# Retention followed by a squared-ReLU FFN: pacing FFN steps by thirds of a chunk in block 0 and by a line of tokens afterwards

## Chip, cores and metric

One Trainium2 chip, one core of it. The metric is the device time of the whole program in microseconds (us). A *ratio* is the mean time of one kernel's fast runs over the mean of the other's fast runs of the same rounds; it is therefore not quite the ratio of the medians that are quoted beside it. Engine names: PE is TensorE (PEld its weight loads), DVE is VectorE, ACT is ScalarE, POOL is GpSimd, SP issues the transfers. The *granted clock* is the share of PE's full clock that the profile records as granted; *half clock* is 0.50. A *bank* is a buffer of the kernel that PE writes, and that another engine has to read before PE may write it again.

## The reference

```python
# attention: batch 8, heads 8, sequence 576, head dim 64
scores = (q @ k.transpose(0, 1, 3, 2)) / sqrt(64)
ret    = scores * where(rel >= 0, gamma ** rel, 0)      # decay per head
x      = (ret @ v).transpose(0, 2, 1, 3).reshape(4608, 512)
# FFN: w_in 512 x 2048, w_out 2048 x 512
h      = maximum(x @ w_in, 0)
out    = (h * h) @ w_out
```

## The kernel before

Three stages overlap in one instruction stream. *Attention* goes in 40 chunks of up to 128 tokens (per batch four of 128 and one of 64). *The first FFN product* goes in 9 blocks of 512 tokens (`TOK`). Block 0 has 16 plain steps (`first_in`), each four products of 128x512; blocks 1 to 8 have 28 steps each (`ffn_in`) of a seven-product scheme that needs sums of x and of the weights. *The second product* (the output product) comes last, alone. The weights arrive as 64-bit floats and are converted on DVE and ACT, six parts per piece, while block 0 runs.

In these traces PE takes its matmuls in the program's order (it idled 5.36 us before T6 below, with an FFN step behind it whose weights were ready), so the program decides where FFN steps stand between the parts of attention. That is what `ffn`, called three times per chunk (once per *third*), does.

```python
def turn(i):        # transposes k and q of chunk i on PE into the t bank, then copies
    p = ps_t.tile([128, 2, 512], F32, tag="t")          # one buffer
    ...                                                 # 16 transposes
    nc.scalar.copy(to, p[...])                          # kT, ACT
    nc.vector.tensor_tensor(to, p[...], dq[...])        # qT, DVE

def scores(i):      # scores into the same t bank, masked by DVE ("ret")
    ...
    nc.vector.tensor_tensor(r[:cs], both[:cs], msk[...], op=ALU.mult)

def retain_c(i):    # last part of attention of a chunk
    ...
    if more:
        grown(i, 1)                                     # state to SBUF, ACT
    ...
    while at < tok + cs:
        n = at // TOK
        while steps and steps[0][0] <= (n - 2 if n > 4 else n - 3):
            step()                                      # forced: x[n] takes this block's room
            owed[0] -= 1
        ...
        nc.scalar.copy(xT[n][...], p[...])              # x to SBUF, ACT: frees x's bank
        ...                                             # a whole block of x queues its steps

def ffn_in(n, mp, j):                                   # step of blocks 1..8
    if j == 0 and mp == 0:
        for f in sums_x[n]:
            f()                                         # x sums that are still due
    ...                                                 # 4 products of 128x256, then DVE, ACT, POOL
    if mp == N_MP - 1 and j in (3, 4, 5) and n_next[0] > n + 1:
        sums_x[n + 1].pop(0)()                          # one x sum of the next block

def ffn(i):                                             # called per third of a chunk
    if tok < TOK + R_0:                                 # R_0 = 640 tokens
        rate = (N_W1 - 2) / R_0 if tok >= TOK else 0
    elif tok < 5 * TOK:
        rate = (3 * N_MP * NP - LAG) / (4 * TOK - TOK - R_0 + TOK)
    else:
        rate = N_MP * NP / TOK
    owed[0] += cs / 3 * rate
    while steps and owed[0] >= 1:
        owed[0] -= 1
        step()

for i in range(N_CH + 1):                               # the part after the first chunks
    retain_a(i - 1); ffn(i - 1); convert(6)
    retain_b(i - 1)
    scores(i);       ffn(i - 1); convert(6)
    turn(i + 1)
    retain_c(i - 1); ffn(i - 1); convert(6)
```

Of the kernel before, what the change touches and what calls it, by code (L numbers as in the profile page):

```python
# [15 lines left out]
C = 128  # L16
CH = C // 2
TOK = 512
# [22 lines left out]
def kernel(  # L41
# [36 lines left out]
    B, H, S, D = q.shape  # L78
# [7 lines left out]
    N_MP = N_M // 2  # L86
    N_MQ = N_M // 2
    N_BLK = n_tok // TOK
    NP = len(PRODUCTS)
    NCH = -(-S // C)  # L90
    chunks = [(b, ci, ci * C, min(C, S - ci * C)) for b in range(B) for ci in range(NCH)]
    N_CH = len(chunks)
# [62 lines left out]
    N_W1 = N_DF  # L155
# [89 lines left out]
    def w_out_parts():  # L245

        for j in range(N_W1, N_W1 + 3):
            yield lambda j=j: fetch_w(j)
        for j in range(N_W1, len(pieces)):
            one, two, beside, three, four, five = round_parts(j)  # L250
            yield one
            yield lambda two=two, beside=beside: (two(), beside())
            yield three
            yield four

            def last(j=j, five=five):
                five()
                fetch_w(j + 3)

            yield last  # L260
            wi, m, e = pieces[j]
            mh, mq = divmod(m, N_MQ)
            if e == 1:

                at = slice(2 * mh, 2 * mh + 2)
                b = [stage[0][:, o, at, :] for o in range(4)] + [stage[1][:, o, at, :] for o in range(3)]
                r1, r2, r3, r4 = right_sums(*b)
                yield lambda r1=r1, r2=r2: (r1(), r2())
                yield lambda r3=r3, r4=r4: (r3(), r4())
            if e == 1 and mh == 1:  # L270

                for st_, at in ((stage[0], slice(0, 4)), (stage[1], slice(4, 7))):
                    yield from right_sums(*(st_[:, :, o, :] for o in range(NP)))
                    yield lambda st_=st_, at=at, mq=mq: nc.sync.dma_start(
                        w2_dram[at, :, mq, :].rearrange("o p f -> p o f"), st_.rearrange("p o s f -> p o (s f)"))
# [4 lines left out]
    def fetch_raw(count):  # L280

        for _ in range(count):
            if n_raw[0] < min(N_W1, n_made[0] + N_RAW):
                fetch_w(n_raw[0])
                n_raw[0] += 1
# [23 lines left out]
    def convert(count):  # L309
        for _ in range(count):  # L310
            f = next(w_in_steps, None)
            f and f()
# [14 lines left out]
    for half in range(2):  # L327
        at = slice(CH * half, CH * half + CH)
# [8 lines left out]
    N_EARLY = TOK // C  # L337
# [76 lines left out]
    def within(i, h):  # L414

        s = st[i]
        b_, ci, c0, cs = chunks[i]
        own, grow = [], []
        for hp, e, b in HEADS:
            own.append(lambda hp=hp, e=e, b=b: nc.tensor.matmul(  # L420
                x_at(hp, b, h), lhsT=s["vs"][rows(h), 2 * hp + b, :], rhs=s["ret"][rows(h), e, hp, :],
                start=clears(b, hp // 2), stop=False, skip_group_check=True))
            grow.append(lambda hp=hp, e=e, b=b: nc.tensor.matmul(  # L423
                u_ps[0][rows(e), hp, :], lhsT=loaded[i][1][rows(1 - h), 2 * hp + e, :], rhs=s["vs"][rows(1 - h), 2 * hp + b, :],
                start=(ci == 0 and h == 1 and hp == 0), stop=(hp == HP - 1), skip_group_check=True))
        return own, grow

    def grown(i, h):
        nc.scalar.copy(u_sb[(2 * chunks[i][1] + h + 1) % 3], u_ps[0])

    def retain_a(i):

        b_, ci, c0, cs = chunks[i]
        xp[0] = ps_x.tile([128, 2, 256], F32, tag="x", name="x_ps", padded_shape=[128, 2, 512])
        clean.clear()
        if ci == 0:
            u_ps[0] = ps_u.tile([128, HP, D], F32, tag="u", name="u_ps")
        if cs < C:
            return
        own, grow = within(i, 1)  # L440
        for j in range(0, len(own), 2):
            for f in own[j:j + 2] + grow[j:j + 2]:
                f()
        grown(i, 0)

    def retain_b(i):

        s = st[i]
        b_, ci, c0, cs = chunks[i]
        for h in reversed(range(cs // CH)):  # L450
            if 2 * ci + h == 0:
                continue
            u = u_sb[(2 * ci + h) % 3]
            for hp, e, b in HEADS[0:2] + HEADS[4:6] + HEADS[2:4] + HEADS[6:8]:
                nc.tensor.matmul(x_at(hp, b, h), lhsT=u[rows(e), hp, :], rhs=s["qT"][rows(e), hp, CH * h:CH * h + CH],  # L455
                                 start=clears(b, hp // 2), stop=False, skip_group_check=True)

    def retain_c(i):

        b_, ci, c0, cs = chunks[i]  # L460
        own, grow = within(i, 0)
        more = ci + 1 < NCH
        if i < N_EARLY or i >= N_CH - 2:

            nc.scalar.copy(u_sb[(2 * ci + (cs // CH)) % 3][:, 0:2, 0:1], xp[0][:, :, cs - CH:cs - CH + 1])
        for j in range(0, len(own), 2):
            for f in own[j:j + 2] + (grow[j:j + 2] if more else []):
                f()
        if more:
            grown(i, 1)  # L470
        tok = b_ * S + c0
        at = tok
        p = xp[0][:, :, 0:256].rearrange("p a (g t) -> p a g t", g=2)
        while at < tok + cs:
            n = at // TOK

            while steps and steps[0][0] <= (n - 2 if n > 4 else n - 3):
                step()
                owed[0] -= 1
            end = min(tok + cs, (n + 1) * TOK)  # L480
            nc.scalar.copy(xT[n][:, :, at - n * TOK:end - n * TOK].rearrange("p (a g) t -> p a g t", a=2),  # L481
                           p[:, :, :, at - tok:end - tok])
            at = end
            if n_next[0] < N_BLK and (n_next[0] + 1) * TOK <= at:
                steps.extend(block_steps(n_next[0]))
                n_next[0] += 1
        st[i] = loaded[i] = None
# [137 lines left out]


    steps = []
    owed = [0.0]
    w_out_steps = w_out_parts()
    n_w2 = [0]  # L630

    def block_steps(n):
        if n == 0:
            return [(0, first_in, j) for j in range(N_W1)]
        return [(n, ffn_in, n, mp, j) for mp in range(N_MP) for j in range(NP)]

    def step():
        n, f, *args = steps.pop(0)
        f(*args)

    n_next = [0]



    R_0 = TOK * 5 // 4
    LAG = 7

    def ffn(i):

        b, ci, c0, cs = chunks[max(0, min(i, N_CH - 1))]  # L650
        tok = b * S + c0
        if tok < TOK + R_0:
            rate = (N_W1 - 2) / R_0 if tok >= TOK else 0
        elif tok < 5 * TOK:
            rate = (3 * N_MP * NP - LAG) / (4 * TOK - TOK - R_0 + TOK)
        else:
            rate = N_MP * NP / TOK
        owed[0] += cs / 3 * rate
        while steps and owed[0] >= 1:
            owed[0] -= 1  # L660
            step()

    turn(0)
    for i in range(N_CH + 1):
        if i <= N_EARLY:

            convert((0, 0, 2, 5, 5)[i])
            if i >= 1:
                retain_a(i - 1)
                retain_b(i - 1)  # L670
                retain_c(i - 1)
            convert((0, 0, 1, 1, 1)[i])
            if i == N_EARLY:
                step()
            scores(i)
            if i == N_EARLY:
                convert(6)
                step()
            turn(i + 1)
            if i == N_EARLY:  # L680
                convert(5)
        else:
            retain_a(i - 1)
            ffn(i - 1)
            convert(6)
            retain_b(i - 1)
            if i < N_CH:
                scores(i)
            ffn(i - 1)
            convert(6)  # L690
            if i + 1 < N_CH:
                turn(i + 1)
            retain_c(i - 1)
            ffn(i - 1)
            convert(6)
        if i + 3 < N_CH:
            load(i + 3)
        if i < N_EARLY:
            fetch_raw(1)
# [210 lines left out]
```

## Time and profile before

| what | before |
|---|---|
| timed median (1019.52 to 1026.13) | 1025.22 us |
| span of the profiled execution | 1019.0 us |
| PE busy / DVE busy | 983.6 / 751.6 us |
| output product starts, lasts | 616.4, 402.6 us |

PE is busy 97% of the span. The prediction below shows the lines that tell where the rest is. One view is added here: DVE in order of time in the worst place, between two attention transposes without an FFN step (start, length in us, work).

```profile
48.07 0.69 DVE L381 TENSOR_TENSOR qT<-t_ps,dq 128x512 f32<-128x512 f32 x1
48.68 0.42 DVE L205 TENSOR_SCALAR w<-w 128x512 uint32<-128x512 uint32 x1
...
50.79 0.69 DVE L223 SCALAR_TENSOR_TENSOR w<-w,w 128x512 uint32<-128x512 uint32 x1
51.40 0.42 DVE L205 TENSOR_SCALAR w<-w 128x512 uint32<-128x512 uint32 x1
...
53.52 0.69 DVE L223 SCALAR_TENSOR_TENSOR w<-w,w 128x512 uint32<-128x512 uint32 x1
54.13 0.68 DVE L406 TENSOR_TENSOR ret<-sc_ps,msk 128x512 f32<-128x512 f32 x1
```

PE had finished the scores at 49.5. The mask that reads them (L406, "ret") starts only at 54.13, behind two weight conversions (each from L205 to L223); and the next transposes need the bank that the mask frees.

### The profile page before, as it was taken

The page shows a single profiled execution, that of the slowest core. Times are in us where ns is not written, and L with a number is a line of the kernel's source. Part 1 is how long each engine was busy: PE and PEld are TensorE (multiplying, and loading weights), DVE is VectorE, ACT ScalarE, POOL GpSimd, SP SyncE. Part 2 cuts the span into 40 slices and gives each one's busy share as a digit, 9 for nine tenths or more (in the row PEclk, how much of TensorE's full clock was granted, in tenths as well). Part 3 has the DMA queues.
Part 4 walks back from the last instruction along what each step waited for, and adds up shares of the span by engine and source line. Part 5 has one row for each costly group of instructions (what it writes and reads, how often), then busy time and mean ns, then how long its engine had stood idle before and what let it go on. Part 6 is the DMA issues. An engine that isn't in the chain of part 4 may idle for free.

```text
span 1019.0 us, 24086 instructions
## 1 busy us (share of the span) xinstructions
PE 983.6 (97%) x10376; PEld 862.1 (85%) x10376; DVE 751.6 (74%) x1418; ACT 184.9 (18%) x425; POOL 80.3 (8%) x82
## 2 busy tenths in 40 slices
PE   6789999999999999999999998999999999999998
PEld 4444488888888788888788888999999999999997
DVE  2679577666888887888886776877777677777765
ACT  2435221111312213212221000000000000000000
POOL 1100001101111011110101000000000000000000
PEclk9789999999999999999999999999999999999999
DMA  8965547737578669669537898784855747565351
GB/s 201 236 191 162 131 154 204 195 122 208 159 241 270 188 227 268 219 211 288 178 146 271 337 420 307 279 288 157 290 201 200 271 167 258 193 232 207 124 207 42
DMA packets 187658, 220.34 MB, mean 216 GB/s; under 512 B 119200, under 2 KB 137632, under 8 KB 178592
## 3 DMA queue, kind: packets, MB, share of 16 engines
q1 hardware_dynamic: 187552, 218.81, 65.8%
q8 instruction: 81, 1.33, 0.5%
q14 instruction: 25, 0.20, 0.1%
HBM read 129.39 MB, written 89.39 MB: 215 GB/s over the span
## 4 chain that ended last, share of the span: by engine, by line
PE 90%; DVE 4%; DMA 2%; SPq 2%; issue 1%; ACT 1%; DVEq 0%; ACTq 0%
PE h_b L578 17%; PE o_b L790 16%; PE h_c L578 11%; PE h_a L578 11%; PE o_c L790 11%; PE o_a L790 11%; PE h_ps L543 5%; PE x_ps L420 3%; PE t_ps L373 2%; PE x_ps L455 2%; PE sc_ps L399 1%; DMA a<-g_dram 1%; DMA k_ld<-in_k_dram 1%; PE u_ps L423 1%; SPq L142 1%
## 5 line engine op out<-in xcount | busy, mean ns | idle before, releaser
L578 PE MATMUL h_b<-room,w 128*128 128x256 f32 x736 | 178.0, 385 | 0.0
L578 PEld LDWEIGHTS h_b<-room,w 128*128 128x128 f32 x736 | 136.5, 190 | 19.9 <-DVE room L597 0.3
L790 PE MATMUL o_b<-w,room 128*128 128x128 f32 x1168 | 144.5, 275 | 0.2 <-DVE room L741 0.2
L790 PEld LDWEIGHTS o_b<-w,room 128*128 128x128 f32 x1168 | 137.2, 192 | 0.5 <-DVE room L741 0.4
L790 PE MATMUL o_c<-w,room 128*128 128x128 f32 x1008 | 123.0, 275 | 0.0
L790 PEld LDWEIGHTS o_c<-w,room 128*128 128x128 f32 x1008 | 117.7, 192 | 0.0
L578 PE MATMUL h_c<-room,w 128*128 128x256 f32 x480 | 115.9, 384 | 0.0
L578 PE MATMUL h_a<-room,w 128*128 128x256 f32 x448 | 106.9, 381 | 0.0
L578 PEld LDWEIGHTS h_c<-room,w 128*128 128x128 f32 x480 | 89.2, 190 | 12.8
L578 PEld LDWEIGHTS h_a<-room,w 128*128 128x128 f32 x448 | 84.3, 190 | 12.2 <-issue 0.5
L790 PE MATMUL o_a<-w,a 128*128 128x128 f32 x688 | 85.9, 275 | 2.6 <-DMA a<-g_dram 2.6
L790 PEld LDWEIGHTS o_a<-w,a 128*128 128x128 f32 x688 | 81.3, 192 | 2.9 <-issue 2.8
L585 DVE SCALAR_TENSOR_TENSOR room<-room 128x512 f32<-128x512 f32 x96 | 69.7, 726 | 3.3
L595 POOL TENSOR_TENSOR room<-room 128x512 f32<-128x512 f32 x32 | 35.9, 1121 | 441.8 <-ACT room L594 358.7
L801 ACT COPY r<-o_a 128x128 f32<-128x128 f32 x54 | 14.4, 266 | 276.9 <-PE o_a L790 246.3
L543 PE MATMUL h_ps<-room,w 128*128 128x512 f32 x128 | 62.7, 636 | 1.0 <-ACT room L481 1.0
L420 PEld LDWEIGHTS x_ps<-ret,v_ld 64*64 64x64 f32 x1152 | 42.4, 143 | 20.1 <-issue 13.6
L597 DVE TENSOR_TENSOR room<-h_b,room 128x512 f32<-128x512 f32 x32 | 22.1, 691 | 50.1 <-PE h_b L578 47.7
L420 PE MATMUL x_ps<-ret,v_ld 64*64 64x64 f32 x1152 | 52.6, 234 | 5.7 <-ACT room L481 1.9
L408 POOL TENSOR_TENSOR v_ld<-v_ld,dv 128x512 f32<-128x512 f32 (+1 forms) x40 | 44.2, 1108 | 90.3 <-DMA v_ld<-in_v_dram 69.7
L543 PEld LDWEIGHTS h_ps<-room,w 128*128 128x128 f32 x128 | 24.5, 201 | 28.0 <-issue 25.7
L588 ACT COPY room<-h_a 128x512 f32<-128x512 f32 x32 | 18.8, 587 | 157.4 <-PE h_a L578 157.4
(94 smaller groups left out, 1361.1 us busy)
## 6 DMA issues: line engine op xcount, KB each, us to landing
g_dram<-room SPq DMA_DIRECT2D x32, 1792.0 KB, 7.3
a<-g_dram SPq DMA_DIRECT2D x43, 1024.0 KB, 6.8
room<-g_dram SPq DMA_DIRECT2D x20, 1024.0 KB, 6.0
w<-w_dram SPq DMA_DIRECT2D x7, 1792.0 KB, 12.2
out_dram<-room SPq DMA_DIRECT2D x18, 512.0 KB, 3.3
v_ld<-in_v_dram SPq DMA_DIRECT2D x32, 256.0 KB, 3.8
w<-in_moe_w_in_dram SPq DMA_DIRECT2D x16, 512.0 KB, 5.0
w<-in_moe_w_out_dram SPq DMA_DIRECT2D x16, 512.0 KB, 3.8
```

Source lines behind the costliest of these rows:

```text
L373: nc.tensor.transpose(p[:, h, j, hp, :], loaded[i][j][rows(h), 2 * hp:2 * hp + 2, :], ident[rows(h), rows(h)])
L408: nc.gpsimd.tensor_tensor(vs[:cs], vs[:cs], dv[:cs, :, ci:ci + 1].to_broadcast([cs, H, D]), op=ALU.mult)
L420: own.append(lambda hp=hp, e=e, b=b: nc.tensor.matmul(x_at(hp, b, h), lhsT=s["vs"][rows(h), 2 * hp + b, :], rhs=s["ret"][rows(h), e, hp, : ...
L455: nc.tensor.matmul(x_at(hp, b, h), lhsT=u[rows(e), hp, :], rhs=s["qT"][rows(e), hp, CH * h:CH * h + CH], start=clears(b, hp // 2), stop=Fa ...
L543: nc.tensor.matmul(p.rearrange("p h t -> p (h t)"), lhsT=w[:, c, :], rhs=xT[0][:, c, :], start=(c == 0), stop=(c == N_DM - 1))
L578: nc.tensor.matmul(p[:, mm, :], lhsT=w[:, c, :], rhs=xs[n][right][:, c, :], start=(j in OPENS and mm == 0 and c == 0), stop=(j in CLOSES a ...
L585: nc.vector.scalar_tensor_tensor(t, t, 0.0, t, op0=ALU.max, op1=ALU.mult)
L588: nc.scalar.copy(p1, p)
L595: nc.gpsimd.tensor_tensor(g["A11"], g["A11"], g["A11"], op=ALU.mult)
L597: nc.vector.tensor_tensor(g["A22"], p, p15, op=ALU.add)
L790: nc.tensor.matmul(p, lhsT=s["lefts"][left][:, m, :], rhs=w_out[j][:, m, WO_SLOT[right], :], start=(i in OPENS and m == 0), stop=(i in CLO ...
L801: nc.scalar.copy(r[:, 0, 0:128], p)
```

## The change

The intent: in block 0 exactly one FFN step and one conversion per third, so that no third is without a step; after that a line of (tokens, steps) points that finishes each block about when its x room is wanted, again with at least one step in each third. The copy of x also goes ahead of the copy of the state on ACT, to free x's bank sooner.

```diff
-        if more:
-            grown(i, 1)
         tok = b_ * S + c0
...
             nc.scalar.copy(xT[n][:, :, at - n * TOK:end - n * TOK]...)
+            if more and at == tok:
+                grown(i, 1)
...
+    THIRD = C // 3
+    PACE = ((4 * TOK + THIRD // 2, N_W1 + 2 * N_MP * NP - 2), (5 * TOK - THIRD, N_W1 + 3 * N_MP * NP - 2),
+            (6 * TOK + THIRD // 2, N_W1 + 4 * N_MP * NP - 2), (8 * TOK + THIRD // 2, N_W1 + 6 * N_MP * NP - 2),
+            (9 * TOK, N_W1 + 7 * N_MP * NP - 2))
...
     def ffn(i):
...                                              (the three rates and `owed` are gone)
+        gone[0] += chunks[max(0, min(i, N_CH - 1))][3] / 3
+        if steps and steps[0][0] == 0:
+            step()
+            return
...                                              (want: the line's value at gone[0])
+        if steps:
+            step()
+        while steps and done[0] < int(want):
             step()
```

More of the change, by code (lines that the diff above doesn't have):

```diff
@@ L478, in retain_c @@
                 step()
-                owed[0] -= 1
             end = min(tok + cs, (n + 1) * TOK)
@@ L627 @@
     steps = []
-    owed = [0.0]
     w_out_steps = w_out_parts()
@@ L638, in step @@
         n, f, *args = steps.pop(0)
+        done[0] += 1
         f(*args)
     n_next = [0]
-    R_0 = TOK * 5 // 4
-    LAG = 7
-    def ffn(i):
-        b, ci, c0, cs = chunks[max(0, min(i, N_CH - 1))]
-        tok = b * S + c0
-        if tok < TOK + R_0:
-            rate = (N_W1 - 2) / R_0 if tok >= TOK else 0
-        elif tok < 5 * TOK:
-            rate = (3 * N_MP * NP - LAG) / (4 * TOK - TOK - R_0 + TOK)
-        else:
-            rate = N_MP * NP / TOK
-        owed[0] += cs / 3 * rate
-        while steps and owed[0] >= 1:
-            owed[0] -= 1
+    THIRD = C // 3
+    PACE = ((4 * TOK + THIRD // 2, N_W1 + 2 * N_MP * NP - 2), (5 * TOK - THIRD, N_W1 + 3 * N_MP * NP - 2),
+            (6 * TOK + THIRD // 2, N_W1 + 4 * N_MP * NP - 2), (8 * TOK + THIRD // 2, N_W1 + 6 * N_MP * NP - 2),
+            (9 * TOK, N_W1 + 7 * N_MP * NP - 2))
+    done = [0]
+    gone = [0]
+    behind = []
+    def ffn(i):
+        gone[0] += chunks[max(0, min(i, N_CH - 1))][3] / 3
+        if steps and steps[0][0] == 0:
+            step()
+            return
+        if not behind:
+            behind.append((gone[0] - THIRD, done[0]))
+        points = behind + [p for p in PACE if p[0] > behind[0][0]]
+        want = points[-1][1]
+        for (x0, y0), (x1, y1) in zip(points, points[1:]):
+            if gone[0] < x1:
+                want = y0 + (y1 - y0) * (gone[0] - x0) / (x1 - x0)
+                break
+        if steps:
+            step()
+        while steps and done[0] < int(want):
             step()
@@ L682 @@
         else:
+            if i == N_EARLY + 1:
+                gone[0] = TOK
             retain_a(i - 1)
```

## The prediction

> **What bounds the kernel now.** I read the page's busy line first, then the table by stage, the waits of the matmul engine (PE), and last its order of time where the waits fall. All times are us from the start of the profiled span of 1019.0 (that execution took 1020.7; the timed median is 1025.22). The page:
>
> ```profile
> PE 983.6 (97%) x10376; PEld 862.1 (85%) x10376; DVE 751.6 (74%) x1418; ACT 184.9 (18%) x425; POOL 80.3 (8%) x82
> PE   6789999999999999999999998999999999999998
> DVE  2679577666888887888886776877777677777765
> PEclk9789999999999999999999999999999999999999
> ```
>
> PE is the bound, and the change gives it not one matmul more or less. So only three things can be won: PE's idle time, PE's time at a lower clock, and small gaps that the busy figure hides. Slices 2 and 3 (25 to 76 us) show a granted clock of 0.7 and 0.8. The table by stage (stretch, its length, busy us of each engine with instruction counts, granted clock, DMA share, GB/s):
>
> ```profile
> 47.40:61.20 13.80, 7.43 (x87) 4.53 (x86) 11.80 (x23) 4.11 (x8) 1.07 (x1) 0.63 0.79 220
> 61.20:111.90 50.70, 48.34 (x572) 24.27 (x570) 39.44 (x64) 22.21 (x43) 4.94 (x4) 1.00 0.55 155
> 111.90:136.20 24.30, 22.91 (x267) 14.90 (x268) 12.43 (x20) 5.80 (x12) 0.00 (x0) 1.00 0.61 161
> 136.20:550.00 413.80, 409.34 (x4993) 341.87 (x4993) 330.35 (x546) 97.03 (x193) 58.67 (x54) 1.00 0.67 205
> 550.00:616.40 66.40, 66.40 (x320) 58.22 (x321) 48.47 (x72) 6.60 (x13) 6.24 (x6) 1.00 0.93 362
> ```
>
> PE idles 6.4 us in the 13.8 us after 47.4, then 2.4, 1.4, 4.5 and 0. The output product (616.4 to the end) is idle some 7.8 us, and the change doesn't touch it; nor does it touch the first 36 us. The worst place, PE in order of time (start, us, work, and in brackets the idle time before it with its releaser):
>
> ```profile
> 46.99 0.42 PE L373 MATMUL t_ps<-ident,q_ld 64*128 64x64 f32 x8
> 47.34 0.46 PE L455 MATMUL x_ps<-qT,u_sb 64*64 64x64 f32 x16
> 48.82 0.69 PE L399 MATMUL sc_ps<-qT,kT 64*64 64x64 f32 x32 [1.01 <-DVE qT L381]
> 54.87 0.69 PE L373 MATMUL t_ps<-ident,k_ld 64*128 64x64 f32 x8 [5.36 <-DVE ret L406]
> 55.92 1.12 PE L420 MATMUL x_ps<-ret,v_ld 64*64 64x64 f32 x16
> ```
>
> Between two transposes (L373) of attention no FFN step stands here. PE finishes the scores, and the mask on VectorE (DVE, L406) that frees their bank waits behind two weight conversions in DVE's order. The waits from 40 to 140 us:
>
> ```profile
> PE t_ps L373 <- DVE ret L406: 6.5, 3, 5.4
> PE x_ps L420 <- ACT room L481: 1.9, 1, 1.9
> PE sc_ps L399 <- DVE qT L381: 1.0, 1, 1.0
> PE x_ps L420 <- ACT w L481: 0.6, 1, 0.6
> ```
>
> The 1.9 (at 88.6) also follows a third without a step: nothing covers the copy of x on ScalarE (ACT). The chain of waits agrees: in 48-54, 68-71 and 86-98 us it runs through DVE's conversions.
>
> **What the Trainium skill says.** "TensorE: Matmul & The Clock Gate", "Part 1: The HAM clock gate", states that PE's clock is halved after an idle window of about 3.4 us. The trace agrees: eight passes of the 128x512 product took 3.63 us at most places, and 5.65 at 57.0, after the 5.36 idle; the stretch's clock is 0.63. The same page's first table gives ACT and DVE strict first-in-first-out queues; the trace agrees in that the ready mask waits behind conversions. "Perfetto Trace Analysis", "Identifying the Most-Contended Engine", warns that matmul busy time is a poor measure of headroom: here weight loads are 83% busy where PE shows 99% (136-550), so some slack per step is hidden, but this change doesn't shorten steps.
>
> **The change part by part.** From the instruction orders of both kernels I counted the FFN steps finished before each attention transpose T (one per chunk). Before: T5 2, T6 2, T7 5, T8 8, T9 10, T10 13, T11 15, T12 20, T13 27. After: 2, 4, 7, 10, 13, 16, 20, 26, 32. The number of matmuls and of places where attention and FFN alternate is nearly equal (1387 groups against 1385), so no switching cost is added.
>
> *1. Block 0: one step per third.* Price of a chunk with three steps: PE 3 x 3.63 = 10.9, plus attention's five parts, about 0.7 + 0.55 + 0.6 + 0.5 + 0.6 = 3.0: 13.9 to 14.0. DVE for the same chunk: three conversions of 2.73 (starts 0.33, 0.34, 0.72, 0.72 and 0.61 apart) = 8.2, three squares of 0.60 = 1.8, mask and qT 1.2, and about 0.9 for the one instruction per chunk that runs long (1.55 instead of 0.68 at 44.5): 12.1. So with three steps PE is the bound; with fewer, DVE sets the pace, which is what before shows.
>
> By hand from 47.4, with durations of the trace and the new order: the third step starts at 47.5 (its weights are done at 47.46) and ends at 51.1; second attention part and scores to 52.2; fourth step, weights done at 51.4, to 55.85. DVE: the fifth conversion's last three instructions need ACT, which is free of the relu at 51.7 and done at 52.95; they end at 55.05, the mask at 55.7, and T6 comes at 55.85, 1.0 later than before but with two more steps behind it and no idle. Then 13.9 per chunk: T7 69.7, T8 83.7, T9 97.7, T10 111.7. Before, T10 stood at 111.92 with 13 steps done; now 16. Gain: 3 x 3.63 + 0.2 = **11.1 us**. Cross-check from the losses: idle 1.01 + 5.36 + 1.85 + 0.36 = 8.6, and 54.9 to 61.2 at half clock, 6.3 x 0.5 = 3.15: together 11.7.
>
> *2. 111.9 to 136.2.* Of the two idle waits (0.82 on the mask, 0.57 on a copy) I count half: 0.7. A new cost: block 1's four x sums now stand in a row at its start, since block 0 ends before x of block 1 is there. The first product needs none of them; by hand the second sum is ready about 114.9, when the second product needs it. Zero, doubtful by 1.
>
> *3. The line by tokens.* Before, two blocks end in a burst of six forced steps with no step after the copy of x; at 507.16 PE idles 1.42, at 379.5 and 383 0.55 and 0.44. After, no burst is longer than three, and a step always follows the copy. I count 1.9 of the 4.5 idle. Against it, three later blocks start with three sums in a row on DVE: 0.3 each, 0.9.
>
> *4. The state's copy to SBUF after x's copy.* It frees x's bank one copy (0.37) sooner and delays the state by 0.6, behind a step: nothing beyond what part 1 counts.
>
> *5. The tail.* About 32 steps stand alone after attention instead of 37; that stretch has no idle time already: nothing.
>
> Sum: 11.1 + 0.7 + 1.9 - 0.9 = 12.8 us.
>
> **The rivals.** *DVE and ACT become block 0's bound.* For: in the new order ACT's conversion of weight piece j+2 stands behind the relu of step j (before, j+4 or j+5), so the lead over PE shrinks. From the end of step j: 0.5 relu, 1.24 for two ACT instructions, 2.1 for three of DVE, so 3.9; step j+2 starts about 5.8 later. Against: those 1.9 us of slack. If I'm wrong by 1 us per third over some 12 thirds, the whole gain but the clock's goes: about 1022. *Idle time merely moves to the next wait*, as in any paced pipeline with one x bank and one transpose bank: half the gain, 1018. *More than counted:* two of three timed runs took 5 us longer than the profiled one; if they hold a further cold stretch at block 0, steady steps remove that too, and it is about 1007. *A transfer is late*, as the weight pieces are wanted 10 us sooner: from 40 to 140 no wait of PE names a DMA, and DMA share is 0.55; little weight.
>
> **Range and chances.** 1025.2 - 12.8 is 1012.4; I say 1012. Low 1005 is the larger gain with the extra cold stretch, high 1019 the half gain. Over 2% faster means below 1004.7, a gain of 20.5. All idle from 36 to 616 is 1.0 + 6.4 + 2.4 + 1.4 + 4.5 = 15.7, and the half clock after 51 adds 3.2: it would need everything and more. 7%. Over 2% slower needs new waits of 33 us: 1%. Within 2%: 92%.
>
> **What would show it.** In the changed profile: no idle above 1 us between 47 and 61, T6 near 55.9 and T10 near 111.7; granted clock 1.00 from about 41 on; the wait of L373 on the mask under 2 us in total from 40 to 140, and none of 1.9 on x's copy; weight conversions never named by PE's waits in block 0; the end of attention's and FFN's stage at about 604 instead of 616; the output product as long as before (402.6). The prediction is wrong if PE's waits in block 0 name conversions (w) or x sums for several us, or if the lower clock stays.

## The result

The changed kernel took 1012.91 us (median; 1010.1 to 1012.96) against 1025.22 before: ratio 0.9885, 95% interval 0.9845 to 0.9924. That is 1.1% faster, within 2%, and 0.9 us from the predicted 1012. The profiled span went from 1019.0 to 1011.3, a smaller step, because the profiled execution of before was one of its fastest.

The page of the changed kernel, the lines that answer to those of before:

```profile
PE 983.6 (97%) x10376; PEld 861.0 (85%) x10376; DVE 752.3 (74%) x1418; ACT 183.4 (18%) x425; POOL 79.8 (8%) x82
PE   5999999999999999999999998999999999999998
PEclk9999999999999999999999999999999999999999
```

PE's busy time is the same 983.6 us, by chance: with equal steps counted it fell by some 3 us from T5 to T10 (the clock), rose by 1.8 before T5 and by some 1.4 from T10 to T39 (not explained). T5 is the transpose of chunk 5, chunks counted from 0, as in the prediction; the "sixth transpose" of the expectations is T6.

The dents in slices 2 and 3 are gone, and so is the clock of 0.8 in slice 3. The 0.7 of slice 2 is no gain: the changed profile has no clock record before 42.7 us, and the page counts a stretch without a record as full clock. The 32 score products of one chunk (L399) took 1.08 us at 28.54 before and 1.08 at 30.68 after, against 0.65 at full clock; both starts ran slow. Its table by stage (stretch, length, busy us of PE, PEld, DVE, ACT and POOL with counts, granted clock, DMA share, GB/s):

```profile
48.10:57.10 9.00, 8.86 (x81) 4.21 (x80) 8.54 (x16) 3.07 (x6) 0.00 (x0) 1.00 0.75 230
57.10:112.80 55.70, 55.45 (x618) 27.91 (x618) 45.77 (x78) 25.19 (x49) 4.85 (x4) 1.00 0.64 178
112.80:136.40 23.60, 23.27 (x289) 19.05 (x288) 19.02 (x31) 6.35 (x13) 2.06 (x2) 1.00 0.65 168
136.40:550.00 413.60, 407.19 (x4968) 339.77 (x4968) 327.98 (x537) 94.56 (x190) 58.76 (x54) 1.00 0.69 213
550.00:608.70 58.70, 58.70 (x300) 51.14 (x299) 42.68 (x64) 5.87 (x11) 5.20 (x5) 1.00 0.89 349
```

The first two rows run from T5 to T6 and on to T10. PE idles 0.14 and 0.25 us in them. From 136 to 550, however, PE now idles 6.4 us where before it was 4.5. In order of time at the old gap:

```profile
48.77 3.70 PE L542 MATMUL h_ps<-room,w 128*128 128x512 f32 x8
52.40 0.46 PE L455 MATMUL x_ps<-qT,u_sb 64*64 64x64 f32 x16
52.68 0.65 PE L399 MATMUL sc_ps<-qT,kT 64*64 64x64 f32 x32
53.26 3.70 PE L542 MATMUL h_ps<-room,w 128*128 128x512 f32 x8
57.12 0.46 PE L373 MATMUL t_ps<-ident,k_ld 64*128 64x64 f32 x8 [0.17 <-DVE ret L406]
```

The two new steps (L542) stand before and after the scores (L399), and the transpose waits 0.17 instead of 5.36. PE's waits of 136 to 620 us:

```profile
PE h_b L577 <- DVE room L505: 3.6, 3, 1.6
PE t_ps L373 <- DVE ret L406: 2.8, 3, 1.3
```

The first is new: a block's second product waits for the second x sum (L505). DVE of the changed kernel in order of time from 372 us shows it:

```profile
372.04 0.55 DVE L242 TENSOR_TENSOR w<-w 128x384 f32<-128x384 f32 x1
372.51 0.68 DVE L505 TENSOR_TENSOR room<-room 128x512 f32<-128x512 f32 x1
373.11 0.68 DVE L506 TENSOR_TENSOR room<-room 128x512 f32<-128x512 f32 x1
373.71 0.68 DVE L507 TENSOR_TENSOR room<-room 128x512 f32<-128x512 f32 x1
```

PE at that time, with its idle time in brackets:

```profile
373.34 1.97 PE L577 MATMUL h_b<-room,w 128*128 128x256 f32 x8 [1.59 <-DVE room L505]
```

The three sums stand in a row, behind other work of the FFN steps in DVE's order, and PE starts when the first of them is done.

How the 7.7 us between the two profiles come about, from the start of each transpose and the steps done by then (a step of 128x256 products, "small", takes 1.73 us, one of 128x512, "large", 3.63):

| stretch | before | after | gain |
|---|---|---|---|
| start to T5 (same work) | 46.7 | 48.1 | -1.4 |
| T5 to T10 | 65.2 us, 11 steps | 64.7 us, 14 steps | 0.5 + 3 x 3.63 = 11.4 |
| T10 to T39 | 415.1 us, 3 large and 176 small steps left in it | 414.2 us, 180 small | 0.9 less 4.0 of work = -3.1 |
| T39 to the output product | 89.4 us, 48 steps | 81.7 us, 44 steps | 7.7 less 6.9 of work = 0.8 |
| output product | 402.6 | 402.6 | 0.0 |

The start lost 1.4 us at the same work: the profile before had a stretch of full clock from 23.5 to 26.9 us and full clock again from 40.6, the changed one from 42.7. The stretches that the change touches make 9.1.

### The profile page after: what moved, and what is told of

It reads as the page before. It is cut to its first block, busy times and chain, and to the rows that moved or that the text cites. A ratio compares the mean times of both kernels' runs of the same rounds, so it can differ in the third digit from the quotient of the medians.

```text
span 1011.3 us, 24085 instructions
## 1 busy us (share of the span) xinstructions
PE 983.6 (97%) x10376; PEld 861.0 (85%) x10376; DVE 752.3 (74%) x1418; ACT 183.4 (18%) x425; POOL 79.8 (8%) x82
## 4 chain that ended last, share of the span: by engine, by line
PE 90%; DVE 5%; DMA 3%; SPq 1%; ACT 1%; issue 0%; DVEq 0%; ACTq 0%
PE o_b L800 16%; PE h_b L577 16%; PE h_c L577 11%; PE o_c L800 11%; PE o_a L800 11%; PE h_a L577 11%; PE h_ps L542 5%; PE x_ps L420 4%; PE t_ps L373 3%; PE x_ps L455 2%; PE sc_ps L399 1%; DMA a<-g_dram 1%; DMA k_ld<-in_k_dram 1%; DVE room L584 1%; PE u_ps L423 1%; SPq L142 0%
## 5 line engine op out<-in xcount | busy, mean ns | idle before, releaser
L577 PEld LDWEIGHTS h_c<-room,w 128*128 128x128 f32 x480 | 89.0, 190 | 12.8
L542 PE MATMUL h_ps<-room,w 128*128 128x512 f32 x128 | 61.6, 626 | 0.7 <-ACT room L478 0.7
L408 POOL TENSOR_TENSOR v_ld<-v_ld,dv 128x512 f32<-128x512 f32 (+1 forms) x40 | 45.2, 1134 | 81.7 <-DMA v_ld<-in_v_dram 74.5
L423 PE MATMUL u_ps<-v_ld,k_ld 64*64 64x64 f32 x1024 | 47.1, 236 | 0.0
L807 DVE TENSOR_TENSOR small<-o_b,small 128x128 f32<-128x128 f32 x63 | 18.3, 291 | 38.5 <-PE o_b L800 38.5
```

What stands on the lines that cost most here:

```text
L408: nc.gpsimd.tensor_tensor(vs[:cs], vs[:cs], dv[:cs, :, ci:ci + 1].to_broadcast([cs, H, D]), op=ALU.mult)
L423: grow.append(lambda hp=hp, e=e, b=b: nc.tensor.matmul(u_ps[0][rows(e), hp, :], lhsT=loaded[i][1][rows(1 - h), 2 * hp + e, :], rhs=s["vs"] ...
L542: nc.tensor.matmul(p.rearrange("p h t -> p (h t)"), lhsT=w[:, c, :], rhs=xT[0][:, c, :], start=(c == 0), stop=(c == N_DM - 1))
L577: nc.tensor.matmul(p[:, mm, :], lhsT=w[:, c, :], rhs=xs[n][right][:, c, :], start=(j in OPENS and mm == 0 and c == 0), stop=(j in CLOSES a ...
L807: nc.vector.tensor_tensor(s["u2"], p, s["p1"], op=ALU.add)
```

## The experiments

Theory A: the gain is made in block 0, nearly all of it in one place, and part of it is clock rather than idle time. Rival B: the line by tokens makes it. Rival D: the clock is beside the point. All kernels below gave correct results.

**e1_block0: block 0's part alone.** In the kernel before:

```diff
-        owed[0] += cs / 3 * rate
+        if steps and steps[0][0] == 0 and i > N_EARLY - 1:
+            step()
+            return
+        owed[0] += cs / 3 * (rate if tok >= TOK + R_0
+                             else (3 * N_MP * NP - LAG) / (4 * TOK - R_0))
```

> The kernel before with one change only: a step per third while block 0's products last; afterwards its own steady rate. Theory A (the gain lies in block 0: idle 8.6 us and half clock 3.2 us gone): T10 near 112 with 16 steps done instead of 13, and a time of 1012 to 1017, so 8 to 13 us under the kernel before in the same rounds; its four rows of x sums at block starts may cost 2 to 5 us of it. Rival B (the gain comes from the line by tokens, which removes forced bursts): within 4 us of the kernel before.

Measured: 1018.5 against 1024.63 us, ratio 0.9943 (0.9925 to 0.9961): 6 us faster, between the two forecasts (theory A had 8 to 13). T5 to T10 took 64.7 us with 14 steps, as in the changed kernel, so block 0's gain is there. What is missing was given back later: T10 to T39 took 418.2 us for 181 small steps, a loss of 5.3 by the accounting above. The waits of 140 to 620 us:

```profile
PE h_b L578 <- DVE room L506: 6.5, 3, 2.4
```

With block 0 finished earlier, the old rate ends blocks before the next block's x is whole: in DVE's instruction order all four x sums stand in a row at the start of blocks 1, 3, 5 and 7. The longest of these waits (2.40 us) was followed by 3.4 us at half clock, from 502.8 on. Rival B falls in its plain form; but the new line is needed to keep what block 0 wins.

**e2_line: the line alone.** In the changed kernel, block 0 was given back its old rate (the same two rates, through `owed`).

```diff
         if steps and steps[0][0] == 0:
-            step()
-            return
+            b, ci, c0, cs = chunks[i]
+            owed[0] += cs / 3 * (old rate of block 0, then of the next blocks)
+            while steps and steps[0][0] == 0 and owed[0] >= 1:
+                owed[0] -= 1
+                step()
+            return
```

> The changed kernel with block 0 paced as before and the line by tokens kept. Theory A: the idle of about 6 us around 49 to 56 us and the waits on x's copy are back, the steady stretch keeps its waits on x sums, so 1023 to 1029, as slow as the kernel before or 1 to 3 us slower. Rival B: near 1013 to 1016.

Measured: 1025.35 against 1024.63 us, ratio 1.0007 (0.9989 to 1.0025). Without block 0's part nothing is won. The 5.3 us wait on the mask was back, and so was the 1.6 on x's copy; its profile also has the 3.6 us of waits on the second x sum that the changed kernel has. Against the kernel before, the line and the order of the copies together are worth nothing measurable; against a rate that runs ahead (e1) they are worth something.

**e5_gap: one place taken back.** The changed kernel without the steps of the first two thirds.

```diff
         if steps and steps[0][0] == 0:
-            step()
+            calls[0] += 1
+            if calls[0] > 2:
+                step()
             return
```

> The changed kernel, but without a step in the first two thirds of block 0, as before; every later third has one. Theory A (this one place holds most of the gain: idle 6.4 us plus about 3 us of half clock): idle of about 5.4 us before the sixth transpose returns, and the time is 8 to 10 us over the changed kernel, 1021 to 1023. Rival E (the gain is spread over block 0's other thirds and the x copies): 3 to 5 us over, about 1017.

Measured, with the unaltered changed kernel (r_after) in the same rounds:

> The changed kernel unaltered, as the yardstick of this call: 1010 to 1014, about 1.2% under the kernel before.

r_after took 1012.88 us (ratio to before 0.9887), e5_gap 1023.0 (0.9988, 0.9968 to 1.0008): 10.1 us apart. In its profile the old gap stands, and no other wait of PE from 40 to 140 us but these two:

```profile
50.28 0.69 PE L399 MATMUL sc_ps<-qT,kT 64*64 64x64 f32 x32 [1.01 <-DVE qT L381]
56.33 0.69 PE L373 MATMUL t_ps<-ident,k_ld 64*128 64x64 f32 x8 [5.36 <-DVE ret L406]
```

The idle is 6.4 us; the time lost is 10.1. Rival E (the gain is spread over block 0; 3 to 5 us) falls. What are the other 3.7? The 10.1 is itself loose: the same kernel (r_gap below) stood at 0.9960 of before instead of 0.9988, which puts the loss near 7.5.

**e6_fill and e8_gap_fill: the clock by itself.** Four products of 128x512 to no purpose, into a bank that nobody reads, go where PE idles. They advance nothing. e6 does it to the kernel before, e8 to e5_gap.

```diff
             if i < N_CH:
                 scores(i)
+            if i == N_EARLY + 1:
+                idle = ps_f.tile([128, 512], F32, tag="f", name="fill_ps")
+                for c in range(N_DM):
+                    nc.tensor.matmul(idle, lhsT=(first piece of w_in)[:, c, :],
+                                     rhs=xT[0][:, c, :], start=(c == 0), stop=(c == N_DM - 1))
             ffn(i - 1)
```

> The kernel before with four products of 128x512 to no purpose (into a bank nobody reads) put where PE idles 5.4 us before the sixth transpose. It advances no work and should lie wholly in idle time. Theory C (that idle also costs clock): the half-clock stretch from 51 to 61 us is gone, the eight passes that follow take 3.6 us instead of 5.65, and the time is 2 to 5 us under the kernel before. Rival D (the idle costs only itself; the clock falls for another reason): the passes still take 5.6, time within 1 us of the kernel before or longer.

> e5_gap with four products to no purpose in the idle time, as in e6. No work is advanced. Theory C: the clock stays, the eight passes after the sixth transpose take 3.6 us instead of about 6, and the time is 2 to 3.5 us under e5_gap of the same rounds. Rival D (clock falls for another reason, or its cost is hidden behind VectorE): within 1 us of it. e6 against the kernel before gave 2 us with an interval that just held zero; this is the second try.

> e5_gap unaltered, as the yardstick of this call: near 1023, with half clock for some 10 us after the idle of 5.4 us.

e6 took 1022.13 against 1024.63, ratio 0.9980 with an interval of 0.9958 to 1.0003: in the direction of theory C, but the interval just holds 1. In its profile T5 to T7 took 22.0 us instead of 24.9. The second pair settles it: e8 1019.37 against r_gap (e5_gap unaltered) 1021.79, medians 2.4 apart; ratios to before 0.9934 (0.9921 to 0.9946) and 0.9960 (0.9946 to 0.9974), which is 2.7 us of the 1026. The intervals touch, but the slowest run of e8 (1020.56) is under the fastest of r_gap (1020.66). PE of r_gap in order of time:

```profile
57.01 0.69 PE L373 MATMUL t_ps<-ident,k_ld 64*128 64x64 f32 x8 [5.36 <-DVE ret L406]
57.49 0.63 PE L373 MATMUL t_ps<-ident,q_ld 64*128 64x64 f32 x8
58.06 1.12 PE L420 MATMUL x_ps<-ret,v_ld 64*64 64x64 f32 x16
59.10 6.38 PE L542 MATMUL h_ps<-room,w 128*128 128x512 f32 x8
```

The same view of e8, where L705 is the fill:

```profile
50.06 3.70 PE L705 MATMUL fill_ps<-room,w 128*128 128x512 f32 x8
55.49 0.46 PE L373 MATMUL t_ps<-ident,k_ld 64*128 64x64 f32 x8 [1.73 <-DVE ret L406]
...
56.74 3.70 PE L542 MATMUL h_ps<-room,w 128*128 128x512 f32 x8
```

The same eight passes take 6.38 us after the idle and 3.70 after the fill; the transposes and the value products in front of them are faster too. T5 to T7 is 25.5 us in r_gap and 22.0 in e8, 3.5 apart; in e5_gap's own profile it is 24.9, 2.9 apart. In the stretch from 48 to 62 us the granted clock is 0.72 and 1.00. So work that is of no use, put into idle time, made the program faster: the idle cost lower clock on top of itself, 2.7 us by the times and 2.9 or 3.5 between profiles. Rival D falls. With 6.4 of idle that makes 9.1 to 9.9, against a loss of 10.1 in one call and some 7.5 in the other; the two parts are shown, their sum only to within these.

**e3_state_first: the order of the two copies undone.**

```diff
+        if more:
+            grown(i, 1)
         tok = b_ * S + c0
...
-            if more and at == tok:
-                grown(i, 1)
```

> The changed kernel with the copy of the state put back ahead of the copy of x. Theory: with a step in every third both copies lie behind a step, so the order is worth nothing: within 1 us of the changed kernel of the same rounds, and no wait on x's copy over 0.5 us. Rival: the order carries part of the gain, and the waits of PE on x's copy return: 2 us or more slower.

Measured: 1013.15 against r_after's 1012.88 (ratios to before 0.9895 and 0.9887). No wait on x's copy appears in its profile. The order of the copies is worth nothing here, because a step covers both.

**e4_sums: x sums sooner.** In the changed kernel:

```diff
-            sums_x[n + 1].pop(0)()
+            while len(sums_x[n + 1]) > 6 - j:
+                sums_x[n + 1].pop(0)()
```

> The changed kernel, but at the sixth product of a block's last group up to three of the next block's x sums that are due are issued, not one, so the second x sum stands two products earlier in VectorE's order. Theory: the 3.6 us that PE waits for that sum (three places, longest 1.6) from 136 us on fall under 1 us, and the time is 2.5 to 4 us under the changed kernel, about 1009 to 1010. Rival: the wait moves to the masks or copies behind the sums, and the time stays within 1 us of 1012.9.

Measured: 1010.39 us, ratio to before 0.9859 (0.9836 to 0.9881), 2.5 us under the changed kernel's median (of another call; the ratios differ by 0.0026 to 0.0028, with overlapping intervals). The profile is clearer than the times. From 136 to 620 us the wait on the sum is gone and the other is as it was:

```profile
PE t_ps L373 <- DVE ret L406: 2.8, 3, 1.3
```

T10 to T39 took 412.0 us instead of 414.2 with the same steps. That is 2.2 us less, but e4's profile has a stretch of half clock in it that the changed kernel's has not, from 478.4 to 481.8, worth an estimated 1.7 (half of 3.4). e7 below has the same sums and no such stretch, and took 410.4. So the row of sums cost the changed kernel 3.9 us.

**e7_fetch: a wait that both kernels have.** The fourth fetch of the last stage stood in SP's queue behind a write that held it 7.26 us; PE waited for that fetch 2.6 us. e4 with the fetch issued earlier:

```diff
-            if n_last in (0, 5, 10):
+            if n_last in (0, 5, 10, 15):
                 fetch_g(n_last // 5)
...
     fetch_w2(NP - 1)
-    fetch_g(3)
```

> The changed kernel with e4's earlier x sums, and the fourth fetch of the last stage issued during the last block, ahead of the write that holds the queue some 7 us. It aims at a wait that both kernels have (2.6 us at 628 to 634) and that in three of six profiles was followed by one window at half clock (1.6 to 2.0 us more in the output product). Expected: the wait gone, the output product about 400 us in every profile, 1006 to 1008, 2.5 to 4 us under e4's 1010.4. Rival: the fetch only takes bandwidth from the transfers beside it, another one becomes late, and the time stays within 1 us of e4.

Measured: 1005.02 us (1004.04 to 1006.84), ratio to before 0.9817 (0.9796 to 0.9839), faster than both kernels by clear intervals, and somewhat under the range expected. The wait on the fetch is gone, and the output product took 400.1 us. This part is not of the change; it shows what was left.

## Why the prediction was right, point by point

*The bound, and what could be won.* Right: no matmul more or less (10376), and the gain is idle time and clock. One reading was loose: the trace shows the clock halved around the gap, but not that it took an idle window of about 3.4 us. The half clock began 1.3 us after PE had stopped (last section). The count that was to exclude a cost of switching (1387 groups against 1385) is in no answer on record: by the traces PE's work changes between attention and FFN (or the output product) 192 times before and 206 after, so a cost of switching is not excluded.

*1. Block 0, 11.1 us.* Right in size and course. T5 to T6 was to take 9.15 us and took 9.0; T5 to T10 was to take 65.0 and took 64.7, both with the steps counted. The absolute times (T6 57.1 for 55.85, T10 112.8 for 111.7) are late by the 1.4 us that this execution had lost before T5. The clock's share, 3.15, was measured at 2.7 (times) and 2.9 to 3.5 (profiles) by the fill. The place was right too: taking back two steps costs 10.1, or some 7.5, of the 11.8 us (1.15% of 1025) of the timed gain. DVE's slack in the rival's chain held; PE's waits in block 0 name no conversion.

*2. From 111.9 to 136.2, 0.7.* The two waits of before are gone, 0.3 us of a wait on the second x sum has come, as the doubt said. From T10 to T12 before took 24.2 us with 3 large and 4 small steps, after 23.7 with 10 small: 0.5 us shorter with 0.5 us less work. So the term was nil, not 0.7.

*3. The line by tokens, +1.9 - 0.9 = +1.0.* **This step failed, sign included.** The predicted removals happened (no 1.42 at a forced burst). But the second term was mis-sized: "three later blocks start with three sums in a row on DVE: 0.3 each" measured 0.46, 1.59 and 1.59, 3.6 in all, and 3.9 by e7's stretch. I had counted the sums alone and not the block's other work that stands in DVE's queue before them. The waits on the mask from 136 us on also grew, from 1.2 to 2.8. Between the profiles T10 to T39 lost 3.1 us. With the sums sooner and no half clock (e7) it gains some 0.7 by the same accounting (410.4 against 415.1, less 4.0 of work). So the sums are all of the loss. Why it is 0.7 then and not the 1.9 that was forecast stays untested; the waits on the mask are as long in e7 (2.8).

*4. The order of the copies, nothing.* Right (e3).

*5. The tail, nothing.* 0.8 us better between the profiles, untested.

*The sum.* 12.8 against 12.3 between the medians, and 11.4 of r_after. The closeness is partly luck: between the profiles the touched stretches make 9.1, and 7.7 with the start. What fills the difference is that typical executions of before were 4.5 us slower than the profiled one (1025.2 against 1020.7). The prediction's rival "more than counted" had seen that; its reason, a further cold stretch at block 0, is not shown. Three things vary between the profiles here: the start (T5 at 46.1 to 48.8 us), the output product (402.5 us, or 404.1 to 405.9 where half clock followed the fetch's wait), and single stretches of 3.4 us at half clock (e1, e2 and e4 have one each). How far these make the 4.5 us was not measured, as timed executions leave only their span and mean clock.

*The view that was to show it.* The granted clock is 1.00 throughout the stretches from T5 on; the wait on the mask from 40 to 136 us is 0.2; FFN's stage ends at 608.7, not at 604, by the 1.4 of the start and the failed third step.

## What to carry to other kernels

Where the matmul engine is the bound and a second, independent stream of matmuls is at hand, put a piece of it into every stretch in which the first stream must wait for another engine; one gap of 6 us cost 7.5 to 10. When such pacing moves work ahead, look again at what was spread over the old positions: here x sums fell into a row at block starts and gave back 3.9 us, and issuing them two products sooner brought it back. Read each part of a change against its own stretch of the trace, as a right total can hold a term of the wrong sign.

## What the Trainium skill lacked or had wrong

- "TensorE: Matmul & The Clock Gate", "HAM oscillation — how this bites in real kernels", gives as a rule no PE idle gaps over about 3.4 us. Shorter ones were followed by half clock here: waits of 2.6 to 3.1 us for the fetch before the output product in 8 of the 11 profiles that have this wait, for 3.4 or 6.8 us, and the output product then took 404.1 to 405.9 us instead of 402.5. In e4's profile even a wait of 1.27 us near 477 us, amid attention's 64x64 matmuls, was followed by it (the same wait in eight other profiles was not, so the length alone does not decide), as its rows by stretches of 2 us show (granted clock third from the right):

```profile
476.00:478.00 2.00, 1.23 (x32) 1.12 (x32) 1.97 (x5) 0.42 (x1) 0.00 (x0) 1.00 1.07 259
478.00:480.00 2.00, 2.00 (x9) 1.60 (x6) 1.40 (x4) 0.52 (x2) 0.00 (x0) 0.60 1.05 207
480.00:482.00 2.00, 2.00 (x32) 1.26 (x34) 0.47 (x1) 0.00 (x0) 0.00 (x0) 0.55 0.43 91
482.00:484.00 2.00, 2.00 (x28) 1.75 (x20) 1.97 (x5) 0.37 (x1) 0.00 (x0) 1.00 0.00 0
```

- The same page, "What's actually happening", has the clock halved after at least one idle window of about 3.4 us. In the kernel before PE stopped at 49.5 us, and the granted clock is 1.00 in the stretch from 49.55 to 50.70 and 0.50 from 50.90 on, so it fell some 1.3 us into the gap. Even with the wait of 1.01 us just before, PE was idle for only 2.3 us by then. In e5_gap it fell 1.4 us into the same gap, in r_gap 2.7.
- No page says that products to no purpose in an unavoidable gap can pay: 2.7 us here (e8 against e5_gap), with the gap's end set by DVE either way.
